# An mLSTM, a token/channel mixer and a gated MLP in one kernel: one shared row tile, merged and differently timed loads, a later end of the output products

## The chip, the cores and the metric

The kernel runs on one core of a Trainium2 chip. The metric is the device time of one execution in microseconds; where runs are compared, the median of several executions is taken.

## What is computed

Three stages follow each other on `B = 2` batches, 768 positions (`S`) and 320 features (8 heads of 40). Cut to what matters:

```python
# 1: mLSTM, a recurrence over t, per batch and head
m_new = max(f[t] + m, i[t]);  C = exp(f[t]+m-m_new) * C + exp(i[t]-m_new) * outer(v[t], k[t])
n = exp(f[t]+m-m_new) * n + exp(i[t]-m_new) * k[t]
y[t] = sigmoid(o[t]) * (C @ q[t]) / max(abs(n @ q[t]), 1)
# 2: mixer
u = x + (relu(x.T @ w_tok1) @ w_tok2).T          # 768 -> 256 -> 768 over positions
x = u + relu(u @ w_ch1) @ w_ch2                  # 320 -> 1536 -> 320 over features
# 3: gated MLP
h = gelu(x @ w_in);  u, v = halves of h          # 320 -> 512 + 512
v = normalise(v) * g_ln;  v_s = w_sg @ v + b_sg  # 768 x 768 over positions
out = x + (u * v_s) @ w_out
```

## The kernel before

**Tiling.** The recurrence is done in chunks of 128 positions, six a batch, twelve in all (`n = 0..11`, `b, c = divmod(n, 6)`). The program first works out all gate terms (`gates`, L424): cumulative sums and running maxima over each 128-position row, 48 rows a batch, one on each partition 64b+16+6h+c. For each chunk there are three steps. `p1(n)` (L523) makes the decay matrix of eight heads in two halves: a matmul of `LR` and `MR` into PSUM bank 0 (L528), an exponential on ScalarE (L529), a triangular mask on GpSimd (L530). `p2(n)` (L533) makes the products of k and q (L540, float32, banks 1 and 2) and multiplies them into the decay matrix on VectorE (L541). `p3(n)` (L543) makes the new state (L563, L567, L571, L575), the old state's share (L554, L555, L581) and the product with v (L583), then the division (L584 to L588). The order in the program is p1(0), p1(1), p2(0), then for each n: p1(n+2), p2(n+1), p3(n), the load of chunk n+3, weights, and the token products of chunk n-1.

**The row tile.** `LR` (L409) holds for each chunk a left operand. It is filled with an indicator (L431, one copy of 128x768 a batch), and 16 of its rows a batch are then overwritten by the gate rows: high and low parts (`uh` L437, `ul` L438) go by four transfers (L441, two a batch) from [row, position] layout into `ust`, and ScalarE copies them into `LR` (L444): for batch 0 chunk 0 by itself and chunks 1 to 5 together, for batch 1 all six at once. In this version each batch has its own part of `LR`.

**Loads of a chunk** (`load_chunk`, L515): one for q (L518, 120 partitions), three for k (L520, 40 partitions each, into zeroed tiles), one for k, v and the output gate by position (L521). All transfers of the kernel are issued from SyncE's queue.

**Weights** come as float64 words and are turned into float32 by one ScalarE (L362) and four VectorE operations (L363, L364, L366, L368) in one of three staging tiles `wt`, then split into a high part (L376, ScalarE) and a low part (L377, VectorE or GpSimd). `wsg` is float32: it is loaded (L395), copied (L396) and subtracted (L397). Tiles of later stages lie at the addresses of tiles of earlier stages.

**Channel stage** (`ch_steps`, L671): steps of eight products (L684 to L689, 384 columns), a relu split (L635, L636), and nine products (L699 to L701, 320 columns) two steps later. **Last stage**: `part_v` (L806), `part_u` (L832), `part_sgu` (L845, 18 matmuls L851 to L853, then L855 to L858) and `part_out` (L863, nine matmuls L867 to L869, added up over d = 0..3 in banks 5, 6, 7, then a residual add L639 and an output transfer L874). `seq` has 16 entries (batch, half, d); entry i's `part_out` stands behind entry i+1's `part_sgu` and `part_u`.

**What sets the order.** Nothing is issued as it is written: every operation goes into a `Plan` (L76), which gives each a modelled duration (`cost`, L103), finds what it depends on by the overlap of regions, gives each a due time (counted back from TensorE's operations, whose due times are the plain sum of their durations), and then schedules all five queues greedily: each engine takes, among the operations that could begin first, the one with the smallest key. TensorE's key is the program order, the others' is the due time less the operation's own length. On SyncE's queue a transfer may start as soon as its place is free and fewer than eight are under way (L216). Operations marked `flex` may go to GpSimd instead of VectorE. `issue` (L264) then emits all in the order of modelled starts; each engine runs its own list strictly in order.

Of the kernel before, what the change touches and what calls it, by code (L numbers as in the profile page):

```python
# [16 lines left out]
ALU = mybir.AluOpType  # L17
# [32 lines left out]
class Op:  # L50
    __slots__ = ("i", "eng", "name", "a", "k", "line", "pre", "suc", "dur", "lat", "start", "end", "due", "lock", "flex",
                 "nbytes", "left", "ready", "key")
# [23 lines left out]
class Plan:  # L76
# [26 lines left out]
    def cost(self, op, outs, ins):  # L103
        name, e = op.name, op.eng
        n = max([elems(outs[0])] + [elems(x) for x in ins[:1]])
        if e == "SP":
            nb = 4
            for _, c in outs[0].ap:
                nb *= c
            op.nbytes = nb  # L110
            return 0.4, 0.0
        if e == "PE":
            if name == "transpose":
                return 0.11, 0.22
            if ins[0].dtype == F32R:
                return max(0.11, 0.00046 * elems(ins[1])), 0.165
            return max(0.224, 0.00184 * elems(ins[1])), 0.165
        if e == "ACT":
            return 0.00083 * n + 0.175, 0.0
        if e == "DVE":  # L120
            big = [x for x in ins if elems(x) > 4 and not in_psum(x)]
            if name == "tensor_scalar" and not in_psum(ins[0]) and n > 16:
                op.lock = True
                return (0.00053 if len(ins) == 1 else 0.00075) * n + 0.14, 0.0
# [4 lines left out]
            return 0.00104 * n + 0.14, 0.0  # L129
        op.lock = True  # L130
        if name == "affine_select":
            return 0.00104 * n + 0.11, 0.0
        if name == "memset":
            return 0.00083 * n + 0.1, 0.0
        return 0.0023 * n + 0.1, 0.0

    def add(self, eng, name, a, k, flex, line):
# [9 lines left out]
        op.lock, op.flex, op.nbytes, op.suc = False, flex, 0, []  # L147
        op.dur, op.lat = self.cost(op, outs, ins)
        pre = set()
# [29 lines left out]
    def order(self):  # L179

        ops = self.ops
        t = 0.0
        for o in ops:
            o.due = 1e9
            if o.eng == "PE":
                t += o.dur
                o.due = t
        for o in reversed(ops):
            tail = 0.0 if o.eng == "PE" else 2.4 + o.nbytes / 3.0e5 if o.eng == "SP" else o.dur
            for s in o.suc:  # L190
                same = s.eng == o.eng
                d = s.due - s.dur - (0.0 if same else o.lat + self.LAT)
                o.due = min(o.due, d)
            o.key = o.i if o.eng == "PE" else o.due - tail
# [4 lines left out]
        def enter(o):  # L199
            avail[o.eng].append(o)  # L200
            if o.flex:
                avail["POOL" if o.eng == "DVE" else "DVE"].append(o)
# [4 lines left out]
        free = dict.fromkeys(avail, 0.0)  # L207
        port = {"DVE": 0.0, "POOL": 0.0}
        lanes, queue, done = [], 0.0, []
        slack = {"PE": 0.05, "ACT": 0.1, "DVE": 0.1, "POOL": 0.1, "SP": 0.05}  # L210

        def begin(o, e):
# [3 lines left out]
            if e == "SP" and len(lanes) >= 8:  # L216
                s = max(s, lanes[-8])
# [5 lines left out]
        while len(done) < len(ops):  # L223
# [27 lines left out]
            if e == "SP":  # L251
                queue = max(queue, free[e] + 1.2) + o.nbytes / 3.0e5
                o.end = queue + 0.6
                lanes.append(o.end)
            done.append(o)
            for q in o.suc:
# [5 lines left out]
        return done  # L262

    def issue(self):  # L264
        for o in self.order():
# [17 lines left out]
def tile_mlstm_mixer_gmlp(  # L283
    ctx: ExitStack,
    tc: tile.TileContext,
    qT_d: bass.AP,
    kT_d: bass.AP,
    kvo_d: bass.AP,
    gates_d: bass.AP,
    con_d: bass.AP,  # L290
    selg_d: bass.AP,
# [13 lines left out]
    for d in (qT_d, kT_d, kvo_d, gates_d, con_d, selg_d, tok1_d, tok2_d, ch1_d, ch2_d, win_d, wsg_d, wout_d,  # L305
# [21 lines left out]
    con = sb("con", CON, 131)  # L327
    nat = sb("nat", NAT, 3840).rearrange("p (b s n) -> p b s n", b=B, s=NC)
    ident, bdm = con[:, 0:128], con[0:120, 128:131]
# [72 lines left out]
    sp.dma_start(out=gates_in, in_=gates_d)  # L402
    sp.dma_start(out=con, in_=con_d)
# [4 lines left out]
    selg = r_gate.take("selg", 360)  # L408
    LR = r_x.take("LR", NC * B * 128, F32R).rearrange("p (n t) -> p n t", n=NC * B)  # L409
# [5 lines left out]
    kTm = [r_cw.take("kTm", 1152)[0:120].rearrange("p (j g t) -> p j g t", j=3, g=3) for _ in range(NSET)]  # L415
    kvo = [r_cw.take("kvo", 1008) for _ in range(NSET)]
    qT = [r_x.take("qT", 384)[0:120].rearrange("p (g t) -> p g t", g=3) for _ in range(NSET)]
    for t in kTm:
        pool.memset(t, 0.0)
    sp.dma_start(out=selg, in_=selg_d)  # L420
# [3 lines left out]
    def gates():  # L424
# [5 lines left out]
        for b in range(B):  # L430
            act.copy(LR[:, 6 * b:6 * b + 6, :], ind6.unsqueeze(2).to_broadcast([128, 6, 128]))  # L431
# [54 lines left out]
        act.copy(selr, selg)  # L486
# [9 lines left out]
        for k in range(3):  # L496
            mm(pd[:, k, :], selg[:, k * 120:(k + 1) * 120], r12, start=True, stop=True)
# [7 lines left out]
    nb_s = [r_x.take("nb", 369)[0:120].rearrange("p (g j e) -> p g j e", g=3, j=3) for _ in range(2)]  # L505
    cd_s = [r_x.take("cd", 369)[0:120].rearrange("p (g j e) -> p g j e", g=3, j=3) for _ in range(2)]
    wv_s = [r_tmp.take("wv", 328).rearrange("p (h e) -> p h e", h=H) for _ in range(2)]
    ct_s = [r_tmp.take("ct", 369)[0:120].rearrange("p (g j e) -> p g j e", g=3, j=3) for _ in range(2)]
# [6 lines left out]
    def load_chunk(n):  # L515
        b, c = divmod(n, NC)
        i = n % NSET
        sp.dma_start(out=qT[i], in_=qT_d[b, c])  # L518
        for j in range(3):
            sp.dma_start(out=kTm[i][40 * j:40 * j + 40, j], in_=kT_d[b, c, j])  # L520
        sp.dma_start(out=kvo[i], in_=kvo_d[b, c * 128:(c + 1) * 128, :])  # L521

    def p1(n):  # L523
        b, c = divmod(n, NC)
        E = E_s[n % 4]
        for hf in range(2):
            p = bank((0,))
            mm(p, LR[:, n, :], MR[b][:, 4 * hf:4 * hf + 4, :], start=True, stop=True)  # L528
# [14 lines left out]
    def p3(n):  # L543
# [12 lines left out]
        if c < NC - 1:  # L556
# [3 lines left out]
            psC = bank((3, 4, 5))[0:120, 0:369].rearrange("p (g j e) -> p g j e", g=3, j=3)  # L560
# [456 lines left out]
```

## Time and profile before, and how to read it

| | |
|---|---|
| device time, median of 3 runs | 373.15 us (373.02 to 373.21) |
| the profiled execution's own time | 376.02 us |
| its span, first to last instruction | 374.3 us |
| TensorE busy | 95% of the span |
| VectorE, ScalarE, GpSimd busy | 71%, 47%, 20% |
| DMA queue busy | 25% of 16 engines |

A row of the timeline reads: start, duration (us), engine, source line, operation, output <- inputs, shape, count, and in brackets the idle time of that engine just before with what ended it. PE is TensorE's matmul, PEld its weight load, DVE VectorE, ACT ScalarE, POOL GpSimd, SPq SyncE's queue. Matmuls are pipelined, so the distance between two starts says what one costs. A releaser is inferred from semaphore events.

### The profile page before, as it was taken

The page shows a single profiled execution, that of the slowest core. Times are in us where ns is not written, and L with a number is a line of the kernel's source. Part 1 is how long each engine was busy: PE and PEld are TensorE (multiplying, and loading weights), DVE is VectorE, ACT ScalarE, POOL GpSimd, SP SyncE. Part 2 cuts the span into 40 slices and gives each one's busy share as a digit, 9 for nine tenths or more (in the row PEclk, how much of TensorE's full clock was granted, in tenths as well). Part 3 has the DMA queues.
Part 4 walks back from the last instruction along what each step waited for, and adds up shares of the span by engine and source line. Part 5 has one row for each costly group of instructions (what it writes and reads, how often), then busy time and mean ns, then how long its engine had stood idle before and what let it go on. Part 6 is the DMA issues. An engine that isn't in the chain of part 4 may idle for free.

```text
span 374.3 us, 5950 instructions
## 1 busy us (share of the span) xinstructions
PE 356.9 (95%) x2257; PEld 344.5 (92%) x2257; DVE 264.7 (71%) x519; ACT 175.8 (47%) x384; POOL 76.2 (20%) x96
## 2 busy tenths in 40 slices
PE   4799999999979999998999999999999999999995
PEld 3599989999959999998999999999999999999994
DVE  2848977998889869889683247675877787454553
ACT  4568765874476364464443234344454344132230
POOL 3234364331430031140040000120012122000000
PEclk9999999999999999999899999999999999999999
DMA  6995895434850014001310000000000010010101
GB/s 189 252 362 172 321 303 171 150 133 139 290 179 0 2 56 161 9 1 48 122 44 0 3 0 0 2 0 3 0 2 0 0 54 0 2 53 3 53 0 54
DMA packets 12456, 31.16 MB, mean 83 GB/s; under 512 B 1676, under 2 KB 6668, under 8 KB 12428
## 3 DMA queue, kind: packets, MB, share of 16 engines
q1 hardware_dynamic: 12428, 30.79, 25.1%
q8 instruction: 18, 0.29, 0.3%
q14 instruction: 10, 0.08, 0.1%
HBM read 28.72 MB, written 1.97 MB: 82 GB/s over the span
## 4 chain that ended last, share of the span: by engine, by line
PE 87%; DVE 5%; ACT 3%; DMA 2%; POOL 1%; issue 1%; SPq 0%; DVEq 0%; ACTq 0%; POOLq 0%
PE ps L699 6%; PE ps L701 6%; PE ps L700 6%; PE ps L540 6%; PE ps L853 5%; PE ps L684 4%; PE ps L852 4%; PE ps L851 4%; PE ps L686 4%; PE ps L685 4%; PE ps L583 4%; PE ps L689 2%; PE ps L688 2%; DMA kTm<-in_kT_dram 2%; PE ps L867 2%; PE ps L868 2%
## 5 line engine op out<-in xcount | busy, mean ns | idle before, releaser
L635 ACT ACTIVATE a<-ps 128x384 fp32r<-128x384 f32 x48 | 23.5, 491 | 44.3 <-PE ps L689 44.2
L636 DVE SCALAR_TENSOR_TENSOR a<-ps,a 128x384 fp32r<-128x384 f32 x48 | 26.5, 554 | 19.7 <-ACT a L635 19.5
L853 PE MATMUL ps<-wsg,v 128*128 128x384 f32 x96 | 32.4, 337 | 0.0
L851 PE MATMUL ps<-wsg,v 128*128 128x384 f32 x96 | 32.3, 337 | 0.0
L852 PE MATMUL ps<-wsg,v 128*128 128x384 f32 x96 | 32.3, 337 | 0.0
L540 PE MATMUL ps<-qT,kTm 120*128 120x128 f32 (+1 forms) x192 | 29.3, 302 | 0.7 <-DMA kTm<-in_kT_dram 0.7
L540 PEld LDWEIGHTS ps<-qT,kTm 120*128 120x128 f32 (+1 forms) x192 | 27.9, 214 | 2.1 <-issue 0.9
L639 DVE TENSOR_TENSOR nat<-ps,nat 128x320 f32<-128x320 f32 x48 | 21.9, 487 | 9.3 <-PE ps L701 5.9
L857 ACT CAST gs<-g 128x384 fp32r<-128x384 f32 x16 | 8.2, 512 | 35.9 <-DVE g L856 35.8
L530 POOL TENSOR_SCALAR_AFFINE_SELECT E<-E 128x512 f32<-128x512 f32 x24 | 16.9, 706 | 36.7 <-ACT E L529 35.6
L799 DVE SCALAR_TENSOR_TENSOR sq<-sq,ps 128x384 f32<-128x384 f32 (+1 forms) x28 | 16.9, 608 | 9.5 <-ACT sq L798 9.3
L583 PE MATMUL ps<-kvo,E 128*128 128x41 f32 x192 | 23.0, 280 | 0.0
L583 PEld LDWEIGHTS ps<-kvo,E 128*128 128x128 f32 x192 | 22.5, 193 | 0.0
L800 ACT ACTIVATE sq<-sq 128x384 f32<-128x384 f32 (+1 forms) x28 | 15.8, 569 | 14.1 <-DVE sq L799 13.9
L541 DVE TENSOR_TENSOR E<-ps,E 128x512 f32<-128x512 f32 x24 | 16.4, 686 | 8.4 <-PE ps L540 7.9
L822 POOL TENSOR_SCALAR mv<-mv 128x1 f32<-128x1 f32 x12 | 2.6, 218 | 93.7 <-DVE mv L821 93.7
L855 DVE SCALAR_TENSOR_TENSOR g<-ps,gln,bsg 128x384 f32<-128x384 f32 x16 | 9.9, 616 | 15.4 <-PE ps L853 15.3
L798 ACT ACTIVATE sq<-ps 128x384 f32<-128x384 f32 (+1 forms) x28 | 14.9, 534 | 11.0 <-PE ps L816 9.2
L853 PEld LDWEIGHTS ps<-wsg,v 128*128 128x128 f32 x96 | 18.0, 188 | 0.3 <-DVE v L826 0.3
L851 PEld LDWEIGHTS ps<-wsg,v 128*128 128x128 f32 x96 | 18.0, 188 | 0.1
L852 PEld LDWEIGHTS ps<-wsg,v 128*128 128x128 f32 x96 | 18.0, 188 | 0.0
L529 ACT ACTIVATE E<-ps 128x512 f32<-128x512 f32 x24 | 14.3, 596 | 4.8 <-PE ps L528 4.6
(334 smaller groups left out, 1143.6 us busy)
## 6 DMA issues: line engine op xcount, KB each, us to landing
kvo<-in_kvo_dram SPq DMA_DIRECT2D x12, 504.0 KB
rwin<-in_win_dram SPq DMA_DIRECT2D x5, 512.0 KB
rwsg<-in_wsg_dram SPq DMA_DIRECT2D x6, 384.0 KB
qT<-in_qT_dram SPq DMA_DIRECT2D x12, 180.0 KB
kTm<-in_kT_dram SPq DMA_DIRECT2D x36, 60.0 KB
out_dram<-nat SPq DMA_DIRECT2D x12, 160.0 KB
rwo<-in_wout_dram SPq DMA_DIRECT2D x4, 320.0 KB
rc__148<-in_ch_dram SPq DMA_DIRECT2D x1, 768.0 KB
```

Source lines behind the costliest of these rows:

```text
L530: pool.affine_select(out=E[:, hf], in_=E[:, hf], pattern=[[0, 4], [1, 128]], compare_op=ALU.is_ge, fill=0.0, base=0, channel_multiplier=-1)
L540: mm(p[:, j, :], kt[0:r, jj, g, :], qt[0:r, g, :], start=True, stop=True)
L583: mm(psO[:, h, :], E[:, h // 4, h % 4, :], v1[:, h, :], start=(c == 0 and h == 0), stop=(h == H - 1))
L635: act.activation(out=hi, in_=p, func=AF.Relu)
L636: dve.scalar_tensor_tensor(out=lo, in0=p, scalar=0.0, in1=asf(hi), op0=ALU.max, op1=ALU.subtract)
L639: dve.tensor_tensor(out=nat[:, b, s], in0=p, in1=nat[:, b, s], op=ALU.add)
L699: mm(acc, a[:, 0, js], w[:, 0, :], start=(m == 0), stop=False)
L700: mm(acc, a[:, 0, js], w[:, 1, :], start=False, stop=False)
L701: mm(acc, a[:, 1, js], w[:, 0, :], start=False, stop=(m == 5))
L851: mm(p, v[:, 0, ds_], wsg[s][:, 0, ts], start=(s == 0), stop=False)
L852: mm(p, v[:, 0, ds_], wsg[s][:, 1, ts], start=False, stop=False)
L853: mm(p, v[:, 1, ds_], wsg[s][:, 0, ts], start=False, stop=(s == NC - 1))
```

## The change

- `LR` has one part for both batches: batch 0's gate rows lie on partitions 0 to 15, batch 1's on 64 to 79, of the same six chunks. One indicator copy is left. p1(n) reads `LR[:, c]`, and so all partitions, whichever batch it is for.
- Batch 0's two row transfers are issued from ScalarE's queue; batch 1's stay on SyncE's.
- q and k of a chunk lie in one tile `qk`; three transfers of 40 partitions bring both (before: one and three). The constant `selg` (180 KB) is no longer loaded but made by a broadcast copy; `con` comes out of the tensor of the gates. `kvo` and `nb`, `cd` change places in memory; `nb` is laid out so that one addition makes it (before: two).
- `p2(1)` uses PSUM banks 6 and 7 in place of 1 and 2.
- In the plan: new modelled durations, due times counted back from the planned ends of TensorE's operations of the round before, up to six rounds of which the one that ends first is kept, the due time itself as key, and a transfer on SyncE's queue may not start more than 9 us ahead of its due time.
- `part_out` of entry 12 to 15 all stand behind the last `part_sgu`.

```diff
@@ cost
+        if name == "dma_start":
...
+            op.wire = nb / (2.0e5 if run < 3000 else 3.1e5 if run < 4096 else 3.9e5)
+            return 0.38, 2.1
...
-            return 0.00083 * n + 0.175, 0.0
+            return 0.00083 * n + 0.175 + 0.1 * scalars, 0.0
...
@@ deadlines, order
-                o.due = t
+                o.due = t if ends is None else ends[o]
...
-            o.key = o.i if o.eng == "PE" else o.due - tail
+            o.key = o.i if o.eng == "PE" else o.due
+    def order(self, ends=None, window=9.0):
...
-            if e == "SP" and len(lanes) >= 8:
-                s = max(s, lanes[-8])
+            if e == "SP":
+                if o.due < 1e8:
+                    s = max(s, o.due - o.dur - window)
+                if len(lanes) >= 8:
+                    s = max(s, lanes[-8])
...
+    def best(self, rounds=6):
+        found, ends = None, None
+        for _ in range(rounds):
+            done, last = self.order(ends)
+            ends = {o: o.start + o.dur for o in done if o.eng == "PE"}
+            if found is None or last < found[0]:
+                found = last, [(o, o.eng) for o in done], {o: (o.start, o.dur, o.end) for o in done}
...
@@ tile_mlstm_mixer_gmlp
-    LR = r_x.take("LR", NC * B * 128, F32R).rearrange("p (n t) -> p n t", n=NC * B)
+    LR = r_x.take("LR", NC * 128, F32R).rearrange("p (n t) -> p n t", n=NC)
...
+    qk = [r_cw.take("qk", 1536)[0:120] for _ in range(NSET)]
+    qT = [t[:, 0:384].rearrange("p (g t) -> p g t", g=3) for t in qk]
+    kTm = [t[:, 384:1536].rearrange("p (j g t) -> p j g t", j=3, g=3) for t in qk]
...
-        for b in range(B):
-            act.copy(LR[:, 6 * b:6 * b + 6, :], ind6.unsqueeze(2).to_broadcast([128, 6, 128]))
+        act.copy(LR, ind6.unsqueeze(2).to_broadcast([128, 6, 128]))
...
-                sp.dma_start(out=ust[64 * b + 8 * j:64 * b + 8 * j + 8],
-                             in_=t[64 * b + 16:64 * b + 64])
+                (act if b == 0 else sp).dma_start(out=ust[64 * b + 8 * j:64 * b + 8 * j + 8],
+                                                  in_=t[64 * b + 16:64 * b + 64])
...
-                act.copy(LR[64 * b:64 * b + 16, 6 * b + cs.start:6 * b + cs.stop, :], ust[64 * b:64 * b + 16, cs, :])
+                act.copy(LR[64 * b:64 * b + 16, cs, :], ust[64 * b:64 * b + 16, cs, :])
...
-        sp.dma_start(out=qT[i], in_=qT_d[b, c])
         for j in range(3):
-            sp.dma_start(out=kTm[i][40 * j:40 * j + 40, j], in_=kT_d[b, c, j])
+            rows = qk[i][40 * j:40 * j + 40]
+            sp.dma_start(out=rows.rearrange("p (w n) -> p w n", w=4)[:, 0:2 + j:1 + j], in_=qk_d[b, c, j])
...
-            mm(p, LR[:, n, :], MR[b][:, 4 * hf:4 * hf + 4, :], start=True, stop=True)
+            mm(p, LR[:, c, :], MR[b][:, 4 * hf:4 * hf + 4, :], start=True, stop=True)
...
-            p = bank((1, 2)).rearrange("p (j t) -> p j t", j=4)
+            p = bank((6, 7) if n == 1 else (1, 2)).rearrange("p (j t) -> p j t", j=4)
...
-                for gs, w in ((slice(0, 2), 3), (slice(2, 3), 2)):
-                    flex.tensor_tensor(out=nb[:, gs, 0:w, :], in0=cd[:, gs, 0:w, :], in1=ct[:, gs, 0:w, :], op=ALU.add)
+                nb8, cd8, ct8 = (t.rearrange("p j g e -> p (j g e)")[:, 0:328] for t in (nb, cd, ct))
+                flex.tensor_tensor(out=nb8, in0=cd8, in1=ct8, op=ALU.add)
...
-        if i:
+        if 0 < i < 13:
             part_out(*seq[i - 1])
-    part_out(*seq[-1])
+    for j in range(12, 16):
+        part_out(*seq[j])
```

## Rows read from the trace of the kernel before

**Rows 1.** Busy time by stretch of 5 us, stretches where TensorE isn't full:

```profile
core 0: us, PE busy (x) PEld busy (x) DVE busy (x) ACT busy (x) POOL busy (x), PEclk, DMA share, GB/s
5.00:10.00 5.00, 4.26 (x18) 3.65 (x17) 0.41 (x1) 1.26 (x3) 0.00 (x0) 1.00 0.84 233
10.00:15.00 5.00, 3.50 (x12) 2.40 (x11) 4.67 (x12) 2.73 (x8) 0.73 (x1) 1.00 0.85 258
15.00:20.00 5.00, 4.13 (x16) 3.36 (x15) 4.64 (x10) 3.65 (x9) 2.32 (x3) 1.00 0.91 278
...
100.00:105.00 5.00, 4.26 (x28) 3.50 (x27) 4.11 (x8) 3.55 (x9) 3.28 (x4) 1.00 0.68 210
105.00:110.00 5.00, 4.61 (x28) 4.35 (x28) 4.13 (x8) 4.86 (x9) 2.70 (x2) 1.00 0.64 194
110.00:115.00 5.00, 3.60 (x21) 3.02 (x20) 4.93 (x9) 2.71 (x5) 0.00 (x0) 1.00 0.12 47
...
175.00:180.00 5.00, 2.97 (x15) 2.68 (x14) 4.16 (x11) 1.31 (x3) 0.00 (x0) 0.88 0.75 254
```

**Rows 2.** Timeline around the stop at 176 us:

```profile
175.14 1.87 SPq L395 DMA_DIRECT2D rwsg<-in_wsg_dram  x4
...
176.19 0.34 PE L689 MATMUL ps<-uT,c__153 128*128 128x384 f32 x1
...
178.08 0.46 ACT L376 CAST wo<-wt 128x320 fp32r<-128x320 f32 x1 [1.02 <-DVE wt L368]
...
178.56 0.39 PE L699 MATMUL ps<-c__158,a 128*128 128x320 f32 x1 [2.03 <-ACT wo L376]
...
182.16 0.36 PE L685 MATMUL ps<-uT,c__214 128*128 128x384 f32 x1
```

**Rows 3.** The same stop, weight loads alone:

```profile
178.53 0.19 PEld L699 LDWEIGHTS ps<-c__158,a 128*128 128x128 f32 x1 [2.32 <-ACT wo L376]
```

**Rows 4.** First and last use of wsg, by line 851:

```profile
L851 PE MATMUL ps<-wsg,v x96: 334/334/422, 263.2 to 366.5; 128*128 128x384 f32 x96
```

**Rows 5.** Timeline of the start:

```profile
5.04 0.82 SPq L441 DMA_DIRECT2D ust<-gt  x1
...
6.48 0.68 SPq L441 DMA_DIRECT2D ust<-gt  x1
...
11.30 1.29 DVE L476 TENSOR_TENSOR MR<-gt,gin 128x512 fp32r<-128x512 f32 x2
...
11.72 0.92 ACT L444 CAST LR<-ust 16x128 fp32r<-16x128 f32 x2 [0.58 <-DMA ust<-gt]
...
12.14 0.77 PE L528 MATMUL ps<-MR,LR 128*128 128x512 f32 x1 [1.36 <-ACT LR L444]
...
21.60 2.66 PE L540 MATMUL ps<-qT,kTm 120*128 120x128 f32 x11
```

**Rows 6.** TensorE alone from 24 us:

```profile
25.11 1.92 PE L583 MATMUL ps<-kvo,E 128*128 128x41 f32 x16
...
55.09 1.96 PE L540 MATMUL ps<-qT,kTm 120*128 120x128 f32 x16
```

**Rows 7.** ScalarE alone, the copy of batch 1's rows:

```profile
24.66 0.83 ACT L444 CAST LR<-ust 16x768 fp32r<-16x768 f32 x1
```

**Rows 8.** Timeline of the end:

```profile
368.01 0.31 PE L868 MATMUL ps<-wo,gs 128*128 128x320 f32 x1
...
368.16 0.31 PE L869 MATMUL ps<-wo,gs 128*128 128x320 f32 x1
...
368.98 0.56 DVE L858 TENSOR_TENSOR gs<-g,gs 128x384 fp32r<-128x384 f32 x1 [0.58 <-ACT gs L857]
...
369.00 0.42 PE L867 MATMUL ps<-wo,gs 128*128 128x320 f32 x1 [0.53 <-ACT gs L857]
```

**Rows 9.** One channel weight's conversion, by its tile:

```profile
L366 DVE SCALAR_TENSOR_TENSOR wt<-rc__148,wt x1: 951/951/951, 86.2 to 86.2; 128x768 int32<-128x768 int32 x1
```

**Rows 10.** VectorE alone, first steps of two channel weights:

```profile
78.29 1.02 DVE L363 TENSOR_SCALAR wt<-wt 128x768 f32<-128x768 f32 x2
```

More of the change, by code (lines that the diff above doesn't have):

```diff
@@ L105, in cost @@
         n = max([elems(outs[0])] + [elems(x) for x in ins[:1]])
-        if e == "SP":
+        scalars = sum(1 for x in ins[1:] if elems(x) <= 1)
+        if name == "dma_start":
+            ap = outs[0] if outs[0].tensor.name not in self.dram else ins[0]
             nb = 4
-            for _, c in outs[0].ap:
+            for _, c in ap.ap:
                 nb *= c
+            run = 4
+            for s, c in reversed(list(ap.ap)[1:]):
+                if s * 4 != run:
+                    break
+                run *= c
             op.nbytes = nb
-            return 0.4, 0.0
+            op.wire = nb / (2.0e5 if run < 3000 else 3.1e5 if run < 4096 else 3.9e5)
+            return 0.38, 2.1
         if e == "PE":
@@ L177, in add, with deadlines @@
         self.ops.append(op)
-    def order(self):
-        ops = self.ops
+    def deadlines(self, ends):
         t = 0.0
-        for o in ops:
+        for o in self.ops:
+            o.eng, o.dur = o.eng0, o.dur0
             o.due = 1e9
@@ L186, in order @@
                 t += o.dur
-                o.due = t
-        for o in reversed(ops):
-            tail = 0.0 if o.eng == "PE" else 2.4 + o.nbytes / 3.0e5 if o.eng == "SP" else o.dur
+                o.due = t if ends is None else ends[o]
+        for o in reversed(self.ops):
             for s in o.suc:
-                same = s.eng == o.eng
-                d = s.due - s.dur - (0.0 if same else o.lat + self.LAT)
+                d = s.due - s.dur - (0.0 if s.eng == o.eng and s.eng != "SP" else o.lat + o.wire + self.LAT)
                 o.due = min(o.due, d)
-            o.key = o.i if o.eng == "PE" else o.due - tail
+            o.key = o.i if o.eng == "PE" else o.due
+    def order(self, ends=None, window=9.0):
+        ops = self.ops
+        self.deadlines(ends)
+        for o in ops:
             o.left = len(o.pre)
@@ L206, in order @@
                 enter(o)
-        free = dict.fromkeys(avail, 0.0)
+        free = dict.fromkeys(avail, 0.8)
         port = {"DVE": 0.0, "POOL": 0.0}
-        lanes, queue, done = [], 0.0, []
+        lanes, queue, done, last = [], 0.0, [], 0.0
         slack = {"PE": 0.05, "ACT": 0.1, "DVE": 0.1, "POOL": 0.1, "SP": 0.05}
@@ L251, in order @@
             if e == "SP":
-                queue = max(queue, free[e] + 1.2) + o.nbytes / 3.0e5
-                o.end = queue + 0.6
+                queue = max(queue, free[e] + 1.3) + o.wire
+                o.end = queue + 0.8
                 lanes.append(o.end)
+                lanes.sort()
             done.append(o)
+            last = max(last, o.end)
             for q in o.suc:
@@ L261, in order @@
         done.sort(key=lambda o: o.start)
-        return done
+        return done, last
+    def best(self, rounds=6):
[5 more added lines that the diff above has]
+                found = last, [(o, o.eng) for o in done], {o: (o.start, o.dur, o.end) for o in done}
+        for o, e in found[1]:
+            o.eng = e
+            o.start, o.dur, o.end = found[2][o]
+        return [o for o, _ in found[1]]
     def issue(self):
-        for o in self.order():
+        for o in self.best():
             at_line(o.line)(getattr(self.real[o.eng], o.name), o.a, o.k)
@@ L496, in gates @@
         for k in range(3):
-            mm(pd[:, k, :], selg[:, k * 120:(k + 1) * 120], r12, start=True, stop=True)
+            mm(pd[:, k, :], asf(selr)[:, k * 120:(k + 1) * 120], r12, start=True, stop=True)
         act.activation(out=decT, in_=pd, func=AF.Exp, scale=-1.0)
```

73 lines of the change are left out of this document (33 added, 40 removed).

## The prediction

> **What bounds the kernel now.** I read busy time by stretches first. TensorE is busy 95% of the span, and in nearly every stretch it is full; the ones where it isn't are the start, the passage from tokens to channels near 100 us, and a stop at 176 us [rows 1]. Only there, and at the end, can time be won, since the number of matmuls stays as it is. Then I read what TensorE waits for in each.
>
> *The stop at 176.* The last product before it starts at 176.19 and costs 0.17, so the next could start at 176.36; it starts at 178.56 [rows 2], 2.2 us late. The releaser named is a copy of `wo`, which L699 doesn't read. That copy ends at 178.08 + 0.46 = 178.54, and the weight load of L699 starts at 178.53 [rows 3], before it ends: it was something else. The SyncE row at 175.14 says what [rows 2]: four transfers of `wsg`, which is used from 263.2 on [rows 4]. The first words of `wsg[0]` are put at columns CW+768 to CW+1536; `c2t[1]` (c__158) lies at CW+1280 to CW+2560. Half of that tile was free at 175.14, and L699 at 178.56 reads the other half. I read this as TensorE waiting for the landing of a transfer that overlaps the tile, 178.5 - 175.14 = 3.4 us after issue. No row shows whether the wait is by whole tile; the addresses and the time fit.
>
> *After the stop* thirteen products (nine of 320 columns, four of 384) take 182.16 - 178.56 = 3.6 us [rows 2]. At 0.15 for 320 columns [rows 8], so 0.18 for 384, they would take 2.07. The granted clock of that stretch is 0.88 [rows 1], so part of it ran at the lower level: another 1.5 us.
>
> *The start.* p1(0) starts at 12.14, released by the copy of batch 0's rows into LR (11.72), with MR's first half ready in the middle of its two operations, at about 11.95 [rows 5]. The six halves of p1 then go one by one through bank 0. p2(1) comes after them: from 21.60, and the first L583 at 25.11 [rows 5, 6], 3.5 us. Its matmuls take 2.66 us for eleven rows; later sixteen take 1.96 [rows 5, 6]. So they run at half speed, though the clock column says 1.00 [rows 1]: in the first 25 us the durations, not that column, show the clock (1.2 GHz).
>
> **The change, part by part.**
>
> 1. *A transfer no more than 9 us ahead of its due time.* `wsg` is due before 263.2 [rows 4]. Counting back its split, copy, transport and the 9 us, I estimate an issue some 15 us before that in the plan's time; with the due times of the first round, which leave out TensorE's waits (some 17 us, the part of the span in which it isn't busy), some 30 us before. Either way it is far after 182, when `c2t[1]` is dead. The wait goes, and so does the slow stretch behind it: -2.2 - 1.5 = **-3.7**. Bounds: 0 (if the wait is another) and -3.7.
>
> 2. *Output products 12 to 15 behind the last part_sgu.* Behind the last part_sgu stand the nine products of entry 14. The last of them starts at 368.16, the next product could start at 368.31, and starts at 369.00, when the last `gs` is there [rows 8]: 0.7 us. The low part of that `gs` is done at 368.98 + 0.56 = 369.54 [rows 8]. Entry 14's nine take 1.32, so part_sgu ended at 366.99, and 2.6 us have to be covered. Three entries are 27 x 0.147 = 4.0 us: covered. What was moved leaves its old place, where TensorE is full. **-0.7**; bounds -0.9 and 0.
>
> 3. *p2(1) in banks 6 and 7.* These banks are free until the first token product. p2(1) then needs only q and k of chunk 1 and an idle TensorE; idle between 5 and 20 us are 0.74 + 1.50 + 0.87 = 3.1 us [rows 1]. Its 3.5 us after 21.60 fall away, and what the idle time doesn't hold, 0.4, stays: **-3.1**. Bounds: 0 (p2(1) pushes p1(0) back by as much) and -6 (below: the clock).
>
> 4. *One LR, row transfers on two queues.* Batch 1's copy (0.83 us, now at 24.66 [rows 7]) must now be done before p1(0), and its two transfers, which stand in SyncE's queue, must have landed. If all lands as now, p1(0) starts 0.83 later. On the other side, batch 0's second transfer was issued at 6.48, 1.4 us after the first [rows 5], with its data there; from ScalarE's queue it goes right behind the first, and one indicator copy is saved. ScalarE is idle there: it sat waiting before 11.72 [rows 5]. Bounds +2 (batch 1's rows, last in SyncE's queue, land 1.2 us later than now) and -0.2 (MR is ready only at 11.95). I take **+0.3**, nearer to the lower end, because fewer bytes (no `selg`) are ahead of the rows.
>
> 5. *Merged loads, one addition in place of two.* VectorE has room over the whole span and SyncE's queue isn't on the path after the start: **0**; if that cover were gone, an addition is under 0.5 us a chunk.
>
> 6. *New plan.* Every queue gets a new order. Where TensorE is full, this changes nothing; between 100 and 115 us TensorE idles 0.74 + 0.39 + 1.40 = 2.5 us while VectorE is busy 13.2 of 15 [rows 1]. I count **0**, between -2.5 and the price of the slower rival.
>
> Sum: -3.7 - 0.7 - 3.1 + 0.3 = **-7.2**. It is made on the profiled execution: span 374.3, so 367.1. That execution took 376.02 in all, the median of the runs is 373.15; I take the difference from the median: **366.0 us**.
>
> *A rule against term 4.* By rows, batch 0's second transfer waits 1.4 us for SyncE's queue. The Trainium skill, "DMA: Bandwidth & Descriptors", section "Issuing engines are not separate DMA queues", says that transfers of all issuing engines run on the same 16 DMA engines and interleave, so that a second issuer saves only issue time. By that rule the rows are no sooner through the backlog, term 4 is +0.8, and the time would be 366.5.
>
> **The rivals.**
>
> *A. The clock comes up early (faster).* With p2(1) behind p2(0), TensorE has some 7 us of matmuls at half speed in a row from 6 us on, before p1(0). The only rise in the rows comes after TensorE was full from 20 to 25 us [rows 5, 6]. If it rises near 12, the six halves of p1 (0.77 each [rows 5], half of it at full speed) shorten by 6 x 0.3 = 1.8, and the products between them by as much again: -3.6 more, 362.4. Against it: p2(1) may be placed in pieces, with idle time between. The Trainium skill, "TensorE: Matmul & The Clock Gate", Part 1, says that the slow clock is the state at rest and that sustained activity lifts it; by that rule this rival has the better case the less p2(1) is broken up.
>
> *B. The start gains nothing.* p1(0) waits for both batches' rows, p2(1) fills the time in front of it, or the plan puts p2(1) ahead of the running-maximum matmuls. Terms 3 and 4 become +0.8: sum -3.6, 369.5. For it: the rows land last behind the chunk loads already now [rows 5].
>
> *C. The stop at 176 stays*, because it isn't the landing of `wsg`, or the due times don't hold it back: sum -3.5, 369.6. So the change wouldn't do what it says.
>
> *D. Slower: held-back weights.* Place: the first channel products, near 100 us, and the second half of the channel weights, near 181. Of each of the three first channel weights L363 (1.02 for two [rows 10]), L364 (of the same size) and L366 (0.95, at 86.2 [rows 9]) are done well before 100 us: 3 x 1.97 = 5.9 us of VectorE. If the transfers come so late that this falls into 100 to 115, VectorE has only 15 - 13.2 = 1.8 free [rows 1]; TensorE then idles 4.1 us more and pays 1.5 at the low clock: 5.6. Twice, at both places: 11.2, sum +4.0, 377.2. It decides from 7.2 us of new waits on. Against it: the plan keeps the round that ends first, and in the first round the due times lie before the real ones by TensorE's waits.
>
> **How the numbers follow.** Forecast 0.40, A 0.20, B 0.18, C 0.07, D 0.15. 0.2% (0.75 us) is about what a measurement of this kernel can tell from no change. The forecast, A, B and C are faster, less 0.03 for a mild form of D that ends level: faster 0.82, same 0.03, slower 0.15. The range reaches from A's 362.4 with most of the 2.5 us near 100 won as well, 360.5, to B and C with the row transfers at their bound of +2, 371.5. Left out are D and the edges, some 2 in 10.
>
> **What would show it.** Right: L395 after 235 us, and no wait of L699 above 0.5 us near 175; no wait before the last L867; L540 of p2(1) before 20 us, and the first L583 by 22. Term 4: p1(0) between 11.9 and 13. A: L528 at full speed before 20 us. B: L583 still near 25. D: L684 or L699 waiting for L376 or L377 near 100 or 181, with VectorE full. Wrong would be the prediction above all if new waits appear in the channel stage, where TensorE is full now.

## The result: faster, by about half of what was forecast

The changed kernel takes 370.32 us in the median of 20 runs (367.97 to 373.36), the kernel before 373.86 (373.02 to 376.42, 20 runs): ratio 0.9902, 95% interval 0.9876 to 0.9927, so 3.7 us less (2.7 to 4.6). The forecast was 7.2 less. One thing must be known of the kernel before: its executions fall into two groups; in one set of 29, 17 took 372.8 to 374.0 us and 12 took 375.0 to 376.1, and the profile that the prediction was worked out from (376.02) belongs to the second. The ratios leave out executions more than 1.5% above the fastest of their kernel (four of run 7, one of run 9, two of run 12), which the medians hold.

**Where the time went.** The changed kernel's profiled execution took 370.32 us (span 368.6). Its lines are some 29 further down: L528 is L557, L540 L569, L583 L612, L636 L665, L684 L713, L699 L728. The steps of a weight's conversion, L362 to L368, are L393 to L399, its high and low part L376 and L377 are L407 and L408, and the load of `wsg`, L395, is L426. I call *lead* how much earlier the same matmul starts than in the profile of before: 4.5 us at 31 us of before's time, 5.2 at 52, 2.4 at 58, 3.2 at 99, 0.5 at 124, 0.6 at 173, 4.4 at 186, 5.5 at the last product. Against this profile of before, then, the start gave more than forecast and the stop at 176 gave what was forecast. But 2.8 us were lost at 50 us and 2.7 in the passage from tokens to channels, where the forecast had nothing.

The changed kernel by stretches of 5 us, the same view as [rows 1] (busy time, then granted clock, DMA share, GB/s):

```profile
5.00:10.00 5.00, 2.82 (x13) 2.72 (x13) 3.32 (x11) 1.12 (x3) 0.00 (x0) 1.00 0.56 179
10.00:15.00 5.00, 5.00 (x33) 4.95 (x32) 1.72 (x5) 3.24 (x9) 0.00 (x0) 1.00 0.69 218
15.00:20.00 5.00, 4.49 (x32) 3.75 (x30) 4.82 (x8) 4.25 (x12) 3.71 (x5) 0.99 0.93 273
20.00:25.00 5.00, 5.00 (x32) 4.86 (x30) 3.45 (x9) 2.94 (x8) 2.67 (x5) 0.67 0.75 233
...
45.00:50.00 5.00, 4.28 (x37) 4.05 (x35) 2.05 (x5) 2.94 (x8) 0.38 (x1) 1.00 0.71 221
50.00:55.00 5.00, 3.43 (x27) 3.34 (x27) 4.90 (x13) 3.01 (x6) 2.89 (x5) 1.00 0.23 72
100.00:105.00 5.00, 4.01 (x24) 3.35 (x23) 4.00 (x6) 4.56 (x11) 1.89 (x2) 1.00 0.91 358
105.00:110.00 5.00, 2.57 (x10) 1.93 (x11) 4.64 (x7) 2.82 (x5) 2.11 (x1) 0.87 0.02 5
110.00:115.00 5.00, 5.00 (x27) 4.90 (x26) 3.92 (x8) 3.10 (x6) 0.00 (x0) 0.79 0.00 0
175.00:180.00 5.00, 5.00 (x34) 5.00 (x33) 1.33 (x3) 0.98 (x2) 0.00 (x0) 1.00 0.30 77
```

To see: TensorE is full at 175, where [rows 1] had 2.97 of 5 us. It now idles 2.3 us between 45 and 55 and 3.4 between 100 and 110, and the granted clock (0.87, 0.79) says that part of the work behind the second stop ran at the lower level.

The stop at 176 is gone, but `wsg` isn't issued after 235 us, which the prediction gave as a sign. The first of its transfers leaves right behind the last product that reads the tile it overlaps:

```profile
176.94 0.31 PE L730 MATMUL ps<-c__154,a 128*128 128x320 f32 x1
...
177.28 7.68 SPq L426 DMA_DIRECT2D rwsg<-in_wsg_dram  x6
```

SyncE's queue waited 33.1 us for that product. The window moves a transfer back in the plan, and so in the order of the queue; on the chip it leaves as soon as its turn comes and what it waits for is done. In the profile of before four transfers were issued from 175.14 to 176.63, ahead of that tile's last product (180.62).

The new stop at 50, from the timelines of ScalarE and TensorE:

```profile
46.13 0.67 ACT L393 ACTIVATE wt<-rw__138 128x512 f32<-128x512 f32 x1 [2.53 <-DMA rw__138<-in_tok_dram]
...
48.23 0.67 ACT L393 ACTIVATE wt<-rw__140 128x512 f32<-128x512 f32 x1 [0.70 <-DMA rw__140<-in_tok_dram]
...
50.94 0.58 ACT L558 ACTIVATE E<-ps 128x512 f32<-128x512 f32 x1
```

```profile
51.57 0.50 PE L557 MATMUL ps<-MR,LR 128*128 128x512 f32 x1 [2.29 <-ACT E L558]
```

TensorE waits for an exponential (L558), but that stands in ScalarE's queue behind two weight conversions, which wait for token weights that were held back (issued at 40.15 and 40.54; before at 16.74 and 18.60); the chain of waits has the second transfer with 7.61 us from 40.54 on. In the passage VectorE's queue is what to read:

```profile
104.07 0.95 DVE L408 TENSOR_TENSOR c__147<-wt,c__147 128x768 fp32r<-128x768 f32 x1
105.05 0.95 DVE L418 TENSOR_TENSOR c__149<-wt,c__149 64x768 fp32r<-64x768 f32 x1
106.04 2.00 DVE L394 TENSOR_SCALAR wt<-wt 128x640 f32<-128x640 f32 x1
108.07 0.49 DVE L395 TENSOR_SCALAR wt<-wt 128x640 int32<-128x640 int32 x1
108.48 0.48 DVE L665 SCALAR_TENSOR_TENSOR hl<-ps,hh 128x320 fp32r<-128x320 f32 x1
```

```profile
109.02 0.64 PE L695 MATMUL ps<-hl,w__141 128*128 128x320 f32 x1 [1.99 <-DVE hl L665]
```

`hl`, for which TensorE waits 1.99 us, stands behind two conversion steps of a weight of the second half, and the first of them takes 2.00 us. It is the work of which the forecast said that a new plan costs nothing.

### The profile page after: what moved, and what is told of

Same layout as the page of the kernel before. It is cut to its first block, busy times and chain, and to the rows that moved or that the text cites. A ratio compares the mean times of both kernels' runs of the same rounds, so it can differ in the third digit from the quotient of the medians.

```text
span 368.6 us, 5947 instructions
## 1 busy us (share of the span) xinstructions
PE 352.0 (95%) x2257; PEld 341.9 (93%) x2257; DVE 263.4 (71%) x507; ACT 172.3 (47%) x383; POOL 84.8 (23%) x100
## 4 chain that ended last, share of the span: by engine, by line
PE 88%; DVE 4%; DMA 3%; SPq 3%; ACT 1%; issue 1%; POOL 1%; ACTq 0%; POOLq 0%
PE ps L730 6%; PE ps L728 6%; PE ps L729 6%; PE ps L612 5%; PE ps L882 5%; PE ps L881 5%; PE ps L880 5%; PE ps L715 4%; PE ps L714 4%; PE ps L713 4%; PE ps L569 4%; PE ps L717 2%; PE ps L718 2%; DMA rw__140<-in_tok_dram 2%; SPq L549 2%; PE ps L898 2%
## 5 line engine op out<-in xcount | busy, mean ns | idle before, releaser
L665 DVE SCALAR_TENSOR_TENSOR a<-ps,a 128x384 fp32r<-128x384 f32 x48 | 26.4, 552 | 23.0 <-ACT a L664 22.7
L569 PE MATMUL ps<-qk 120*128 120x128 f32 (+1 forms) x192 | 29.4, 302 | 0.9 <-DMA qk<-in_qk_dram 0.9
L569 PEld LDWEIGHTS ps<-qk 120*128 120x128 f32 (+1 forms) x192 | 28.6, 217 | 1.8 <-issue 1.0
L612 PE MATMUL ps<-kvo,E 128*128 128x41 f32 x192 | 23.6, 282 | 0.1
L612 PEld LDWEIGHTS ps<-kvo,E 128*128 128x128 f32 x192 | 23.0, 194 | 0.3 <-DVE E L570 0.2
L681 DVE TENSOR_TENSOR uT<-ps,uT 128x384 fp32r<-128x384 f32 x24 | 13.3, 553 | 8.6 <-ACT uT L680 8.3
L558 ACT ACTIVATE E<-ps 128x512 f32<-128x512 f32 x24 | 14.3, 595 | 3.8 <-PE ps L557 3.0
```

What stands on the lines that cost most here:

```text
L569: mm(p[:, j, :], kt[0:r, jj, g, :], qt[0:r, g, :], start=True, stop=True)
L612: mm(psO[:, h, :], E[:, h // 4, h % 4, :], v1[:, h, :], start=(c == 0 and h == 0), stop=(h == H - 1))
L665: dve.scalar_tensor_tensor(out=lo, in0=p, scalar=0.0, in1=asf(hi), op0=ALU.max, op1=ALU.subtract)
```

## The experiments

Edits of the order move operations in the finished plan (`shift(ops, which, before)`), and everything else keeps its place; where the plan is made anew, that is said. Names like `second_hl` stand for the operations picked. Each run was timed beside runs of before; its ratio to them needn't be that of the medians. A ratio is turned into microseconds with 373.7, the median of before.

| kernel | median us | ratio to before (95%) |
|---|---|---|
| the change | 370.32 | 0.9902 (0.9876 to 0.9927) |
| 1 before, wsg later | 371.75 | 0.9946 (0.9926 to 0.9966) |
| 2 before, late output products | 372.87 | 0.9976 (0.9951 to 1.0002) |
| 3 token weights earlier | 370.74 | 0.9911 (0.9882 to 0.9939) |
| 4 hl first | 368.27 | 0.9859 (0.9834 to 0.9885) |
| 5 both | 367.62 | 0.9850 (0.9822 to 0.9878) |
| 6 window of 25 us | 371.61 | 0.9928 (0.9901 to 0.9956) |
| 7 old banks | 377.49 | 1.0051 (1.0018 to 1.0084) |
| 8 p2(1) late | 373.11 | 0.9971 (0.9945 to 0.9997) |
| 9 all rows from SyncE | 372.04 | 0.9935 (0.9908 to 0.9962) |
| 10 conversion behind a | 367.93 | 0.9819 (0.9784 to 0.9855) |
| 11 and all rows from ScalarE | 367.11 | 0.9801 (0.9761 to 0.9840) |
| 12 start, alone | 368.77 | 0.9830 (0.9785 to 0.9875) |
| 13 start, on top of 11 | 367.67 | 0.9809 (0.9771 to 0.9847) |

Before, unchanged, was also profiled once more:

> Before, unchanged, profiled once more. Question: does the half clock behind the stop at 176 belong to every execution? Theory (it doesn't; the first profile lay 2.2 us above the median because of it): near 373.3 us, the stop at 176 is there with a wait of about 2.2 us, the granted clock from 175 to 185 is above 0.95 and the thirteen products behind the stop take some 2.1 us instead of 3.6. Rival (the 373 and the 376 us executions differ elsewhere, at the start or in the passage): the slow stretch is there, 0.78 to 0.88, although the time is near 373.3. If the execution is near 375.8, it tells nothing.

It took 376.03 us, again of the second group, with 0.90 and 0.76 at 175 to 185, and so couldn't answer. Its row of L699 does name a releaser, the `wsg` transfer. Run 2 comes closest to an answer.

**1. Before, wsg alone later.**

```diff
+for line, at in ((397, 227.2), (396, 226.0)):   # copies and subtractions, 4 us apart
+    ...
+ops = shift(ops, lambda o: o.line == 395 and "wsg" in tile_of(o), lambda o: o.start >= 215.0)
```

> Before, in its own order; only the six transfers of wsg and their copies and subtractions stand later (planned at 215 and from 226 on, not near 165). TensorE's order is unchanged. Theory (the stop at 176 is TensorE waiting for a wsg transfer that overlaps a tile of the channel weights): no wait above 0.5 us near 175 to 179, granted clock full from 175 to 185, the time 2.0 to 4.0 us less than before. Rival (the stop has another cause, a copy or a bank): a wait of about 2 us stays near 176 or appears within 10 us of it, and the time is within 1 us of before.

The stop is gone, and the clock is full; the four transfers are issued from 177.59 on, behind the tile's last product (177.25), as in the change:

```profile
175.00:180.00 5.00, 5.00 (x34) 5.00 (x33) 4.34 (x12) 1.89 (x5) 0.00 (x0) 1.00 0.28 69
180.00:185.00 5.00, 5.00 (x33) 5.00 (x33) 2.90 (x9) 1.33 (x3) 0.00 (x0) 1.00 0.84 280
```

The lead grows by 3.8 us there (0.3 to 4.1), as in the change. Yet the runs give only 0.0054 x 373.7 = 2.0 us (1.3 to 2.8). The cause of the stop is shown; its price depends on which execution one looks at (two of the eleven of before beside it were of the second group).

**2. Before, output products 12 to 15 last, planned anew by before's own rules.**

```diff
-        if i:
+        if 0 < i < 13:
             part_out(*seq[i - 1])
-    part_out(*seq[-1])
+    for j in range(12, 16):
+        part_out(*seq[j])
```

> Before, with the output products of entries 12 to 15 behind the last part_sgu, nothing else. Theory: the wait of 0.7 us before the last L867 goes and nothing takes its place; 0.6 to 0.9 us less than before. Rival (the last gs, its low part or the eviction of more products sets the end): 0 to 0.3 us.

0.9 us less, though the interval (-1.8 to +0.1) just takes in none; in the profile the lead rises from 1.96 to 2.81 at the end, 0.85. This profile (span 371.2) also holds what the first one hid, the stop at 176 without the low clock:

```profile
178.12 0.38 PE L699 MATMUL ps<-c__158,a 128*128 128x320 f32 x1 [2.29 <-DMA rwsg<-in_wsg_dram]
...
180.22 0.34 PE L685 MATMUL ps<-uT,c__214 128*128 128x384 f32 x1
...
175.00:180.00 5.00, 2.71 (x17) 2.42 (x16) 3.46 (x10) 1.24 (x3) 0.00 (x0) 1.00 0.88 294
```

The releaser named is the `wsg` transfer. And the thirteen products behind it take 180.22 - 178.12 = 2.10 us, where [rows 2] had 3.60. So the 1.5 us of low clock are not in every execution: both profiles of the second group have them, this one doesn't, and ten of the 17 executions of the first group have a mean granted clock of 0.999 or 1.000. I read the median of before as free of them. That is not shown for the other seven of the 17 (mean clock 0.986): where their clock was low, no profile tells.

**3 to 5. The two new stops, one by one and together.**

```diff
+ops = shift(ops, lambda o: o.eng == "SP" and tile_of(o).split("__")[-1] in ("138", "140"), lambda o: o.start >= 24.1)   # 3, 5
+ops = shift(ops, lambda o: o is second_hl, lambda o: o is l394)   # 4, 5: ahead of L394 in VectorE's queue
```

> After, in its own order; only the transfers of the token weights rw__138 and rw__140 stand earlier in SyncE's queue, right behind rw__136. Theory (held-back weights cost the lead won at the start: ScalarE waits for the two transfers and TensorE stops for 2.3 us at 49 to 52): L393 no longer waits for a DMA above 0.3 us, the stop at 49 to 52 falls under 0.5 us, the lead over before at 60 us rises from 2.4 to 4.5 or more, and the time falls by 2.0 to 3.0 us against after, unless the passage to the channels takes it back. Rival (the passage near 100 to 110 us is bound by VectorE, so a lead won ahead of it is lost in it): the stop goes, the waits of TensorE between 99 and 112 grow by about as much, and the time is within 0.7 us of after.

> After, in its own order; only VectorE's second hl (L665) of the passage stands ahead of L394 and L395 on the first half's wt. Theory (the stop of 1.99 us before L695 at 109 is the order of VectorE's queue, L394 at 2.00 us beside POOL's L421 among it): the wait falls under 0.5 us, the granted clock between 105 and 115 is above 0.9, the time is 2.0 to 3.5 us less than after. Rival (VectorE's work as a whole is the bound there, and only the name of the wait changes): waits of 1.5 to 2 us of TensorE appear within the next 8 us (for uT, nat, a or a weight's subtraction), and the time is within 0.7 us of after.

> After with both: the two token weights' transfers earlier and the second hl ahead of L394. Theory (two stops, each with its own cause): both gains add up, 4.0 to 6.0 us less than after, near 365. Rival (the passage is bound by VectorE): not more than the better of the two alone, within 1.5 us of after.

In run 3 the stop at 50 goes and the lead at 99 us is 4.1 (the change: 3.2). At 124 it is 0.2, and the time is that of the change: the rival holds.

```profile
50.00:55.00 5.00, 5.00 (x43) 4.88 (x41) 4.82 (x10) 2.48 (x6) 2.83 (x4) 1.00 0.55 165
100.00:105.00 5.00, 3.72 (x20) 2.77 (x18) 4.90 (x7) 4.67 (x9) 1.37 (x3) 1.00 0.73 264
105.00:110.00 5.00, 2.88 (x11) 2.56 (x12) 4.67 (x8) 2.63 (x6) 1.76 (x1) 0.72 0.01 3
110.00:115.00 5.00, 5.00 (x21) 4.90 (x20) 3.27 (x6) 2.09 (x5) 0.00 (x0) 0.60 0.00 0
```

What was won at 50 is waited away again behind VectorE, which is nearly full (9.6 of 10 us). In run 4 one operation moved brings 0.0043 x 373.7 = 1.6 us (2.0 by the medians): the wait of L695 is gone, the clock stays at 1.00 from 100 to 115, but a wait for `a` follows it, so that both sides were half right:

```profile
109.88 0.44 PE L713 MATMUL ps<-uT,c__145 128*128 128x384 f32 x1 [1.50 <-DVE a L665]
```

With both moves (run 5) the lead of 4.4 at 99 us is still 3.5 at 124. The time, 1.9 us under the change (2.7 by the medians), is a little under run 4's; the sum of 4 us or more that the theory wanted isn't there, and the difference between runs 4 and 5 is well inside their intervals.

**6. A window of 25 us, planned anew.**

```diff
-    def order(self, ends=None, window=9.0):
+    def order(self, ends=None, window=25.0):
```

> After, planned with a window of 25 us in place of 9, so every queue is ordered anew. Theory (weights that are held back too long cost the token stage and crowd VectorE in the passage): the token weights are issued before 30 us, L393 and L394 of the first channel weights' first half lie partly ahead of 88 us, no stop above 1 us at 46 to 53, TensorE idles under 2.6 us between 99 and 112, no stop near 175; 1.5 to 3.5 us less than after. Rival (VectorE's order in the passage is accidental, and each new plan draws another one): within 1.5 us of after, either side, with a new wait of 1 us or more in the passage that has another name.

The rival holds. The stops at 50 and 175 are gone and the lead at 64 us is 5.3, but at 124 it is -1.8. TensorE idles 2.7 us between 55 and 100 and 4.4 between 100 and 115 (the change: 3.4). The new plan put the conversion of the same second-half weight ahead of `a`, and this time L395 took 2.15 us.

```profile
108.16 2.15 DVE L395 TENSOR_SCALAR wt<-wt 128x640 int32<-128x640 int32 x1
110.35 0.83 DVE L397 SCALAR_TENSOR_TENSOR wt<-rc__151,wt 128x640 int32<-128x640 int32 x1
111.21 0.82 DVE L399 SCALAR_TENSOR_TENSOR wt<-rc__151,wt 128x640 int32<-128x640 int32 x1
111.95 1.02 DVE L665 SCALAR_TENSOR_TENSOR a<-ps,a 128x384 fp32r<-128x384 f32 x2
```

TensorE waits 3.4 us for that `a` (L713). Of the 7.1 us of lead lost, 4.9 went between 64 and 99, where no single wait accounts for it, and 2.2 in the passage (the change: 2.7). So earlier transfers didn't free the passage; what stands ahead of `a` in VectorE's queue held it up here too.

**7. p2(1) in banks 1 and 2, planned anew.**

```diff
-            p = bank((6, 7) if n == 1 else (1, 2)).rearrange("p (j t) -> p j t", j=4)
+            p = bank((1, 2)).rearrange("p (j t) -> p j t", j=4)
```

> After, with p2(1) in banks 1 and 2 as before, and planned anew. Theory (the banks are worth the start, 2.3 to 4.8 us of lead at 31 us): the first L612 of chunk 0 is at 21 us or later, the lead over before at 31 us falls to between -1 and 1.5; 1.5 to 3.5 us more than after, unless the passage takes it. Rival (the passage takes the lead anyway): the lead at 31 us falls, the one at 124 us doesn't, and the time is within 0.7 us of after.

Inconclusive for the price, since the plan is another. The first L612 is at 21.98, but the lead at 31 us is 2.6, above the theory's 1.5. The profile took 380.75 us and is one of the four executions that the ratio leaves out; it loses most of what it costs over the change from 64 to 77 us, where the lead falls from 1.8 to -5.5 (granted clock 0.50 from 70 to 75), and that needn't hold for the others. Its start still tells two things:

```profile
12.30 0.47 PE L557 MATMUL ps<-MR,LR 128*128 128x512 f32 x1
...
17.21 0.49 PE L569 MATMUL ps<-qk 120*128 120x128 f32 x2 [2.00 <-DVE E L570]
```

In banks 1 and 2 p2(1) must wait, 2.00 us here, until VectorE has multiplied what p2(0) left there. And p1 ran at full speed (0.47) although p2(1) stood behind it. Run 8 asks for the price with the order kept.

**8. p2(1) behind p1 again, order kept.**

```diff
+p2 = [o for o in ops if o.eng == "PE" and o.line == 569][8:16]
...
+ops = shift(ops, lambda o: o in p2 or o.line == 549 and 14 < o.start < 16, lambda o: o.eng == "PE" and o.start >= 19.5)
```

> After, in its own order; only p2(1) stands behind p1 and p2 of chunk 2 again (its first multiplication on VectorE and the next loads into its buffer behind it). Theory (p2(1) ahead of p1(0) keeps TensorE at work from 7.8 us on, and the start is won by the clock coming up at 13 and not at 25 us): the granted clock's first rise is 3 us or more later, and the lead over before at 31 us falls from 4.5 by 2.5 or more; 1.5 to 3 us more than after, if the passage doesn't take it. Rival (filled idle time alone): the rise stays near 13, idle time before 20 us grows by 2 us. Second rival (p2(1) is worth little, the new order of the start is): lead within 1 us of after's.

The theory holds for the price: 0.0069 x 373.7 = 2.6 us more than the change (1.2 to 3.9), and the lead at 31 us falls from 4.5 to -0.7. In the profiles the difference lies in the length of p1's matmuls, first of this run, then of the change:

```profile
13.31 0.77 PE L557 MATMUL ps<-MR,LR 128*128 128x512 f32 x1
...
16.69 0.73 PE L557 MATMUL ps<-MR,LR 128*128 128x512 f32 x1
```

```profile
13.97 0.49 PE L557 MATMUL ps<-MR,LR 128*128 128x512 f32 x1
...
18.37 0.50 PE L557 MATMUL ps<-MR,LR 128*128 128x512 f32 x1
...
21.85 0.77 PE L557 MATMUL ps<-MR,LR 128*128 128x512 f32 x1
```

Before had 0.77 [rows 5]. In the change TensorE is busy without a gap from 7.8 to 16.8 us, and the granted clock's first record of full speed is at 13.1, ahead of p1(0); in run 8 it is at 28.2. All nine profiles with p2(1) placed as in the change have the first L557 at 0.48 or 0.49, the four of before's order have it at 0.76 or 0.77. But that p2(1) standing in front is what brings the clock up is not shown: TensorE is busy without a gap from 8.5 to 14.5 in run 8 and from 8.1 to 14.3 in run 7, both with p2(1) behind p1(0), and p1(0) runs at half speed in the one and at full speed in the other. TensorE's idle time in the first 30 us hardly differs: 7.7 us before, 7.0 in the change, 7.8 in run 8.

**9 to 11. The row transfers, and VectorE's order once more.**

```diff
+        if o.eng == "ACT" and o.name == "dma_start": o.eng = "SP"      # 9
+ops = shift(ops, l394_l395_of_rc151, lambda o: o is l397_of_rc151)    # 10, 11, on top of 5
+for o in rows_of_batch_1: o.eng = "ACT"                               # 11
```

> After, in its own order; batch 0's row transfers from SyncE's queue again, right ahead of batch 1's. Theory (the queue is worth only issue time; p1(0) waits for batch 1's rows, which stand behind them): batch 0's rows are issued at 7.5 to 8.5 us in place of 4.3 and 5.6, batch 1's about 1.3 us later than in after, p1(0) at 15 or later; 0.3 to 1.3 us more than after. Rival (p1(0) is set by MR and the copies): p1(0) within 0.3 us of 13.97, no difference.

> After with the two token weights' transfers earlier, the second hl ahead of L394, and now L394 and L395 of the passage behind both a (L665) as well. Theory (the rest of the loss in the passage is again VectorE's order: the kernel with the first two moves still waits 1.50 us for a, which stands behind L394 at 1.61 us beside POOL's L421): the wait falls to about 0.5 us, L394 no longer runs beside POOL and takes about 0.5 us, 0.7 to 1.2 us less than with two moves, near 366.6. Rival (VectorE's work as a whole is the bound): a new wait of 0.8 us or more for c__152 or uT before 116 us, and within 0.4 us of the kernel with two moves.

> After with the three moves (token weights' transfers, hl, L394 and L395 behind a) and all four row transfers from ScalarE's queue. Theory: batch 1's rows land 1 to 2 us sooner than 11.45, p1(0) starts at 12.5 to 13.5, and the time is 0.5 to 1.2 us below the kernel with the three moves alone, about 366. Rival (ScalarE's own copies and the landing of the rows are not what p1(0) waits for, or the two extra issues delay ScalarE): within 0.4 us of it.

Run 9: 1.2 us more than the change (1.7 by the medians), which the intervals don't tell from none. p1(0) is at 14.29, only 0.3 later than in the change; in the profile the rest of the lost lead lies in two waits behind it (1.40 us for `qs`, 0.81 for an exponential) and in the clock (0.57 from 20 to 25, 0.75 from 25 to 30). Batch 0's rows, issued from 7.68 on in place of 4.25 and 5.57, are copied at 11.05 in place of 10.13. In run 10 both sides were half right:

```profile
107.52 0.45 PE L713 MATMUL ps<-uT,c__145 128*128 128x384 f32 x1 [0.55 <-DVE a L665]
...
111.79 0.71 PE L728 MATMUL ps<-c__152,a 128*128 128x320 f32 x3 [0.71 <-ACT c__152 L407]
```

The wait for `a` falls from 1.50 to 0.55 and one of 0.71 for `c__152` takes its place; the median is about that of run 5, the ratio 1.2 us lower, inside the intervals. That fits the rival's view that VectorE's work as a whole is now the bound. Run 11 beats both kernels: 367.11 us, 0.9801 of before. Against run 10 its gain isn't outside the intervals. Batch 1's rows are in LR at 11.00 in place of 12.11, but p1(0) starts at 13.53 in place of 13.78: as the rival had it, p1(0) doesn't wait for the rows.

**12 and 13. The waits ahead of the clock's fall at 20 us.**

```diff
+ops = shift(ops, kvo_1_and_rw132, lambda o: o is third_load_of_qk_2_first)   # SyncE's queue
+ops = shift(ops, lambda o: o is l393_of_rw132, lambda o: o.eng == "ACT" and o.start >= 16.4)
```

> After, in its own order; only kvo of chunk 1 and rw__132 are issued ahead of chunk 2's q and k, and ScalarE's L393 of rw__132 stands behind the third and fourth exponential of p1. Theory (the half clock from 18 or 20 us on follows TensorE's waits at 15 to 19 us, of about 0.5 to 1.4 us in all, which come from VectorE waiting for kvo and ScalarE for rw__132; it gives back a part of the start's gain): idle time of TensorE between 15 and 20 us falls under 0.3 us, the clock stays at full from its first rise on, the lead over before at 31 us is 5 or more, and the time falls by 1.5 to 3.5 us against after. Rival (the clock falls back there whatever TensorE does): the idle time goes, the half clock is still there for 3.4 or 6.8 us, and the time is within 0.8 us of after.

> The kernel with the three moves and all rows from ScalarE's queue, and with it the same change of the start. Theory: as for the other, 363 to 365.5. Rival: within 0.8 us of the kernel without it (367.1).

Run 12 is 2.7 us faster than the change by the ratios (1.6 by the medians), the size that the theory gave, but not for its reason: the wait of 0.46 us for `qs` at 17 us stayed, and the clock fell again.

```profile
15.00:20.00 5.00, 4.47 (x31) 3.70 (x31) 4.56 (x7) 3.73 (x11) 3.84 (x5) 0.98 0.87 238
20.00:25.00 5.00, 5.00 (x31) 4.86 (x30) 3.84 (x9) 3.33 (x10) 2.33 (x5) 0.67 0.58 202
```

On top of run 11 the same edit brought nothing. One execution of run 12 (365.67 us) and one of run 11 (363.28) had a mean granted clock of 0.999 and 1.000, so the fall doesn't come every time; what sets it off stays open.

## Why the prediction was half right and half wrong

Two steps failed: term 1, the price of the stop at 176, was too large by 1.7 us, and term 6 put the new plan at nothing, where it costs some 1.9. Together with the 0.5 that term 3 was too large, that is a little more than the miss of 3.5.

By ratios, the parts measured alone are: `wsg` 2.0 us, the late output products 0.9, p2(1) 2.6, together 5.5; the order in the passage with the held-back token weights takes 1.9 back (run 5). That leaves 3.6, and the change gave 3.7. That the two are so close is luck: each part is known only to 0.8 to 1.4 us either way, and terms 4 and 5 were not measured alone.

- **Term 1 (-3.7): right in cause, too large for the median.** The wait for the landing of a `wsg` transfer is shown by run 1 and named in run 2. The mis-sized part is its 1.5 us of low clock: that was in the profile I worked from, and run 2's profile, 3.0 us shorter, has the stop without it. I then took 2.87 us off for the distance between that profile and the median, and so counted the same time twice. By the runs the term is 2.0. How the wait goes was wrong as well: `wsg` isn't held back until long after the tile is dead, but leaves 0.3 us behind its last product, since its place in the queue is behind it.
- **Term 2 (-0.7): right**, 0.9 in the runs, 0.85 in the profile. It was covered: no wait stands before the last products.
- **Term 3 (-3.1): near in size (2.6), wrong in mechanism; that the size came out near is luck.** I had p2(1) fill 3.1 us of idle time; the idle time fell by 0.7. In the profile the gain is the clock that is up before p1(0), rival A's sign (L528 at full speed before 20 us). What brings it up stays open (runs 7 and 8). A's 3.6 us on top didn't come in full: the clock falls back at 20 us, and 0.67 over 5 us gives away 1.65.
- **Term 4 (+0.3): the place was wrong.** p1(0) starts at 13.97, outside the 11.9 to 13 given and 1.8 later than before, near the bound of +2. But it wasn't the rows: batch 1's copy is done at 11.54 + 0.83 = 12.37, 0.2 after before's p1(0), and TensorE had p2(1) to do until 13.97.

```profile
11.54 0.83 ACT L473 CAST LR<-ust 16x768 fp32r<-16x768 f32 x1 [0.48 <-DMA ust<-gt]
```

- **The rule weighed there.** The Trainium skill, "DMA: Bandwidth & Descriptors", section "Issuing engines are not separate DMA queues", lets a second issuer save issue time alone. Run 9 agrees in direction: from SyncE's queue the rows are issued some 3 us later, and copied only 0.9 us later. My reading of it, that they would be no sooner at all, was too strict by that 0.9.
- **Term 5 (0):** no experiment separates it.
- **Term 6 (0): wrong, and the second half of the miss.** The new plan costs 1.9 us or more. It is rival D in a mild form and partly at its place (the first channel products), but in the passage not by its cause: the weight that L394 converts at 106.04 had been issued at 77.24. In the token stage it was late transfers (run 3). In the passage what decides is which of VectorE's operations stand ahead of `hl` and `a`. I had seen VectorE busy 13.2 of 15 us there, and should have priced its order from both sides, as I did its waits.
- **Rivals B and C fall:** the first L612 is at 17.89, and the stop at 176 is gone.

## What to carry to other kernels

When the profile at hand is dearer than the median of the runs, ask which of its stretches makes the difference before subtracting it: a saving that lies in that very stretch is gone from the median already. A limit in a plan's time sets an order and not a time: look where the transfer was really issued. A gain won ahead of a passage where another engine is full is waited away in it (run 3), until that engine's order is put right (run 5). After a new plan, look first at the operations without a near due time that stand ahead of what TensorE waits for.

## What the runs showed of the hardware

- **VectorE beside GpSimd.** The same L394 takes 0.48 us alone and 2.00 beside GpSimd's L421:

```profile
106.04 2.00 DVE L394 TENSOR_SCALAR wt<-wt 128x640 f32<-128x640 f32 x1
...
112.16 0.48 DVE L394 TENSOR_SCALAR wt<-wt 128x640 f32<-128x640 f32 x1
...
105.58 2.11 POOL L421 TENSOR_TENSOR c__150<-wt,c__150 64x768 fp32r<-64x768 f32 x1 [3.61 <-ACT c__150 L419]
```

  The first ends at 108.04, 0.35 after GpSimd's end (107.69); in run 5 it takes 1.61 and ends at 106.90, again 0.35 after GpSimd's (106.55). So it waits for nearly all of the other engine's instruction (times on GpSimd are rough). Not every operation does: L665 at 101.00, which reads PSUM, takes its usual 0.49 beside GpSimd's L408 (100.08 to 101.93). The Trainium skill, "SBUF — State Buffer", section "SBUF: two separate sides", says that GpSimd shares a port pair with VectorE operations in a two-port mode (and, where GpSimd reads SBUF, with those of two SBUF inputs), and that whichever starts first holds it for its whole instruction while the other blocks fully. The rows agree with the blocking; in which mode L394 ran, no row shows.
- **The clock after a stop.** Two stops of about the same length end differently: behind the 2.2 us at 176 the granted clock fell in both profiles of before (0.88 and 0.78; 0.90 and 0.76), behind the 2.5 us of run 2 it stayed at 1.00. The fall costs 1.5 us.
